# FFN pieces between the pieces of a recurrence, and a weight conversion moved between batch elements

## The chip, the cores and the metric

One core of a Trainium2 chip runs the whole program. The metric is the device time of one execution in microseconds (us). Where a ratio is given, it is the mean time of one kernel's fast runs over the mean of the other's fast runs of the same rounds, so it is not quite the ratio of the medians quoted beside it. On this one-core program a run counts as slow when it is over 1.5% above the fastest of its kernel.

One remark on reading the granted TensorE clock. The profile records its changes, and the first record lies some way into the profiled run; what comes before prints as 1.00. So the mean clock of a whole run is good to a few hundredths only.

## The reference, cut to what matters

```python
# 4 batch elements, 8 heads, 768 time steps, head size 40
for t in range(S):
    y[:, :, t] = einsum('bhd,bhde->bhe', r_t, state)
    Sa = einsum('bhde,bhe->bhd', state, a_t)
    state = state * w_t - einsum('bhd,bhe->bhde', Sa, b_t) + einsum('bhd,bhe->bhde', v_t, k_t)
x = y as (3072 tokens, 320)
h = x @ w_in                                  # 320 -> 2048
out = (h * clip(h + 3, 0, 6) / 6) @ w_out     # 2048 -> 320
```

A recurrence over time, then a feed-forward network (FFN) on each token.

## The kernel before

The kernel takes time in 6 groups of 128 steps. For each group and each of the 4 batch elements it does `prepare` (inputs turned, scaled, masked products), one `invert` for all four (a chain of small VectorE instructions), `off_diagonal`, then per element `step` (the state) and `outputs`, which ends in `yg`, the element's 128 finished tokens. An FFN of those tokens follows. The FFN weights arrive as float64 and are rounded to float32 on VectorE and GpSimd in 36 pieces; I call that the conversion.

The parts that matter here:

```python
def rounded(dst, n, loads):                       # one piece of the conversion
    raw = tmp.tile([P, DM, 2], U32, name="raw", tag="yg", bufs=2)   # yg's buffers!
    buf = ffn.tile([P, 3, DM], U32, name="parts", bufs=1)
    # ... DMA into raw, then 5 VectorE and 3 GpSimd instructions; the last, on GpSimd:
    nc.gpsimd.tensor_tensor(out=dst, in0=mf, in1=xf, op=ALU.mult)

def outputs(g, q, o):
    # ...
    yg = tmp.tile([P, NPR, P], F32, name="yg", tag="yg", bufs=2)

os_ = prepared(0)                # prepare x 4, invert, off_diagonal x 4
with behind():                   # everything in here gets a far lower priority
    load_weights()
for g in range(NG):
    def recur(q):
        step(q, os_[q])
        xt = outputs(g, q, os_[q])
        with behind():
            feed_forward(g, q, xt)
    if g + 1 < NG:
        os_ = prepared(g + 1, recur)     # recur(q) before each prepare(g + 1, q)
    else:
        for q in range(B):
            recur(q)
```

The framework builds each engine's instruction order from these priorities. I call that the built order; the prediction shows a wait of 39.8 us that VectorE's built order explains.

Of the kernel before, what the change touches and what calls it, by code (L numbers as in the profile page):

```python
# [15 lines left out]
P = 128  # L16
HP = 64
L = 32
NC = P // L
BEHIND = 1 << 20  # L20
# [10 lines left out]
def kernel(  # L31
# [147 lines left out]
    def load_weights():  # L179
        wi, wo = moe_w_in.bitcast(U32), moe_w_out.bitcast(U32)  # L180
        for i in range(2):
            for f in range(0, DFF, WC):
                rounded(win[:, i, f:f + WC], WC, [
                    (slice(p, p + n), wi[x:x + n, 2 * f:2 * (f + WC)])
                    for p, x, n in FEATURES[i]
                ])
        for f in range(0, DFF // 2, WC):
            rounded(win2[:, f:f + WC], WC, [
                (slice(i * SLOT + p, i * SLOT + p + n),
                 wi[x:x + n, i * DFF + 2 * f:i * DFF + 2 * (f + WC)])  # L190
                for i in range(2) for p, x, n in FEATURES[2]
            ])
        for j in range(NJ):
            rounded(wout[:, j, :], DM, [(slice(0, P), wo[j * P:(j + 1) * P, :])])

# [49 lines left out]
    def prepare(g, q, fc):  # L245
        o = {}
# [8 lines left out]
        wt = turn_pairs(WN)  # L255
        wv = wm[:].rearrange("p (r m i) -> p r m i", m=2, i=HP + 1)
# [25 lines left out]
        at = scaled(AN, gam, grp, "at", tag="at")  # L282
        bt = scaled(BN, rgam, tmp, "bt", tag="turned", bufs=4)
        kt = scaled(KN, rgam, tmp, "kt", tag="turned", bufs=4)
        o["at"] = at
# [3 lines left out]
        for n in range(NPR):  # L289
            nc.tensor.transpose(out=rg[:, n, :], in_=rgam[:, n, :], identity=ident[:])  # L290
        rgt = tmp.tile([P, H, D], F32, name="rgt", bufs=1)
# [17 lines left out]
        for pr in range(NPR):  # L309
            for s in range(2):  # L310
                rows = slice(SLOT * s, SLOT * s + D)
                nc.tensor.matmul(out=f[s][:, pr, :], lhsT=at[rows, pr, :], rhs=bt[rows, pr, :],
                                 start=True, stop=True)
        for s in range(2):
            for c in range(NC):
                cr = slice(c * L, (c + 1) * L)
                nc.scalar.activation(
                    out=fc[cr].rearrange("p (n s) t -> p n s t", s=2)
                    [:, q * NPR:(q + 1) * NPR, s, :],
                    in_=f[s][cr, :, cr], func=AF.Copy, scale=-1.0,  # L320
                )
                if c:
                    nc.scalar.activation(out=ft[cr, 4 * s:4 * s + 4, 0:c * L],  # L323
                                         in_=f[s][cr, :, 0:c * L], func=AF.Copy)
# [4 lines left out]
        masked(E, kt, at)  # L329
        ev = ps_any([P, H, D])  # L330
        for h in range(H):
            nc.tensor.matmul(out=ev[:, cross(h), :], lhsT=E[:, h % 2 * 4 + h // 2, :],  # L332
                             rhs=VN[:, cross(h), 0:D], start=True, stop=True)
        EV = grp.tile([P, H, D], F32, name="EV", tag="EV")
        nc.scalar.activation(out=EV[:], in_=ev[:], func=AF.Copy)
        o["EV"] = EV
        return o
# [31 lines left out]
    def off_diagonal(q, o):  # L369

        ft = o["F"]
        for s in range(2):
            wp = ps_any([P, 4, LW])
            for pr in range(NPR):
                nc.tensor.matmul(out=wp[0:LW, pr, :], lhsT=ft[:, 4 * s + pr, :],  # L375
                                 rhs=tinv[:, q * H + 2 * pr + s, L:P], start=True, stop=True)
            nc.scalar.activation(out=ft[0:LW, 4 * s:4 * s + 4, :], in_=wp[0:LW], func=AF.Copy)

# [6 lines left out]
    def step(q, o):  # L385
# [4 lines left out]
        for j in range(2):  # L390
            nc.tensor.transpose(out=sp[:, j, :],
                                in_=st[:, 2 * j:2 * j + 2, :].rearrange("p r d -> p (r d)"),
                                identity=ident[:])
        S = grp.tile([P, 2, P], F32, name="S", tag="S", bufs=2)
# [5 lines left out]
        for pr in range(NPR):  # L400
            for s in range(2):
                rows = slice(SLOT * s, SLOT * s + D)
                nc.tensor.matmul(out=rp[s][:, pr, :], lhsT=o["at"][rows, pr, :],  # L403
                                 rhs=st[rows, pr, 0:D], start=True, stop=True)
        for s in range(2):
            def places(x):
                return x[:].rearrange("p (n s c) e -> p n s c e", n=2, s=2)[:, :, s]
            nc.vector.tensor_tensor(
                out=places(R), in0=rp[s][:].rearrange("p (n c) e -> p n c e", n=2),
                in1=places(o["EV"]), op=ALU.add)  # L410

# [3 lines left out]
        for h in range(H):  # L415
            nc.tensor.matmul(out=up[:, cross(h), :], lhsT=tinv[:, q * H + h, :],  # L416
                             rhs=R[:, cross(h), :], start=(h == 0), stop=False,
                             skip_group_check=True)
        for c in range(NC):
            cr = slice(c * L, (c + 1) * L)  # L420
            if c:
                for h in range(H):
# [8 lines left out]
        for name, by in (("K", o["V"]), ("B", U)):  # L431
            for pr in range(NPR):
                for s in range(2):
# [5 lines left out]
                    )  # L439
        ssum = tmp.tile([P, NPR, D], F32, name="ssum")  # L440
# [4 lines left out]
    def outputs(g, q, o):  # L445
# [7 lines left out]
        RT, VT, UT = turned(RN), turned(o["V"]), turned(o["U"])  # L453
        m = {}
        for name, x in (("K", VT), ("B", UT)):
            m[name] = next_score()
            masked(m[name], x, RT)
        yg = tmp.tile([P, NPR, P], F32, name="yg", tag="yg", bufs=2)
        y = [ps_acc([P, 2, P]) for _ in range(2)]
        for c in range(2):  # L460
            for name in ("K", "B"):
                for n in range(2):
                    for s in range(2):
# [5 lines left out]
                            start=(name == "K" and n == 0), stop=False)  # L469
        for n in range(2):  # L470
            for s in range(2):
                for c in range(2):
# [4 lines left out]
                        rhs=RT[rows, 2 * n + s, :], start=False, stop=(n == 1))  # L477
        for c in range(2):
# [12 lines left out]
        return xt  # L491


    def feed_forward(g, q, xt):
# [3 lines left out]
        def expand(j0):  # L498

            hp = [bank("h", [P, NQ, P], 2) for _ in range(2)]  # L500
            for kt_ in range(2):
                for half in range(2):
                    for i in range(NQ):
# [4 lines left out]
                                         stop=False)  # L508
            for i in range(NQ):
# [5 lines left out]
            gts = []  # L515
# [7 lines left out]
            return gts  # L523

        def contract(j0, gts):
            for half in range(2):
                for i in range(NQ):
# [3 lines left out]
                                     stop=(j0 == HJ - NQ and half == 1 and i == NQ - 1))  # L531

        last = None
        for j0 in range(0, HJ, NQ):
            gts = expand(j0)
            if last:
                contract(*last)
            last = (j0, gts)
        contract(*last)
# [5 lines left out]
    @contextmanager  # L545
    def behind():

        p = tc.cur_priority
        tc.cur_priority = p + BEHIND
        yield  # L550
        tc.cur_priority = p

    def prepared(g, before=None):
        fc = inv.tile([P, NH, L], F32, name="fc")
        os_ = []
        for q in range(B):
            if before:
                before(q)
            os_.append(prepare(g, q, fc))
        invert(fc)  # L560
        for q, o in enumerate(os_):
            off_diagonal(q, o)
        return os_

    os_ = prepared(0)
    with behind():
        load_weights()
    for g in range(NG):
        def recur(q):
            step(q, os_[q])  # L570
            xt = outputs(g, q, os_[q])
            with behind():
                feed_forward(g, q, xt)

        if g + 1 < NG:
            os_ = prepared(g + 1, recur)
        else:
            for q in range(B):
                recur(q)
# [30 lines left out]
```

## Time and profile before

Before: 1406.8 us, the median of 3 runs (1405.1 to 1414.5); profiled span 1411.0. The span is best cut where an element's `yg` is done. "FFN" is the number of FFN matmuls started in a stretch, times their durations at full clock (0.223, 0.142 and 0.55 us for the three kinds, as in the prediction).

| stretch of the profiled run | us | granted clock | FFN, us at full clock |
|---|---|---|---|
| start to first `yg` | 225.2 | 0.62 | 0 |
| to the first `yg` of group 1 | 162.4 | 0.80 | 40.5 |
| rest of group 1 | 109.0 | 0.72 | 12.5 |
| groups 2 to 4 | 587.0 | 0.81 | 163 |
| group 5 | 164.0 | 0.91 | 74 |
| tail, FFNs alone | 163.4 | 1.00 | 147 |

The columns are start:end, length, busy us and records of PE, PEld, DVE, ACT and POOL, then granted clock, DMA share and GB/s:

```profile
225.20:387.60 162.40, 154.67 (x1368) 134.87 (x1368) 74.11 (x142) 41.84 (x104) 23.47 (x58) 0.80 0.15 26
496.60:1083.60 587.00, 551.90 (x4695) 476.69 (x4693) 265.78 (x486) 159.31 (x405) 77.28 (x200) 0.81 0.16 29
```

PE is busy 552 of 587 us in the middle, and yet runs there at a clock of 0.81.

### The profile page before, as it was taken

How to read it: one execution, taken by the hardware profiler on the slowest of the kernel's cores; microseconds unless marked ns; L12 is line 12 of the kernel's file. 1: busy time of each engine (PE TensorE's matmuls, PEld its weight loads, DVE VectorE, ACT ScalarE, POOL GpSimd, SP SyncE). 2: the span in 40 equal slices, each digit the busy share in tenths (PEclk: the TensorE clock that was granted, in tenths of full speed). 3: DMA queues.
4: the chain of work that ended last, by engine and by line, in shares of the span. 5: the costliest groups of instructions: out<-in, count | busy, mean ns of one | idle time of the engine just before them, and what ended most of it. 6: DMA issues, size and time to landing. Idle time of an engine off the chain costs nothing. (4 is left out here: it accounts for less than half of the span.)

```text
span 1411.0 us, 24203 instructions
## 1 busy us (share of the span) xinstructions
PE 1214.1 (86%) x10032; PEld 1041.7 (74%) x10032; DVE 582.2 (41%) x1113; ACT 327.2 (23%) x805; POOL 248.1 (18%) x503
## 2 busy tenths in 40 slices
PE   5732725999999998999999999898998999999998
PEld 4632615887888877888778888788787877777776
DVE  6577543337333474442733337433327312111111
ACT  2211200222322223322232221322222311111111
POOL 6455563111111111111111111111101000000000
PEclk9555656669957899886877759976999989899999
DMA  5221321221022210222102111011111000000000
GB/s 94 60 56 53 85 75 34 35 35 30 15 35 35 35 30 15 35 38 36 30 10 35 33 29 30 17 33 29 30 23 28 7 6 11 11 17 16 10 10 10
DMA packets 169885, 44.30 MB, mean 31 GB/s; under 512 B 155953, under 2 KB 165169, under 8 KB 169777
## 3 DMA queue, kind: packets, MB, share of 16 engines
q1 hardware_dynamic: 169776, 42.76, 15.1%
q8 instruction: 79, 1.29, 0.4%
q14 instruction: 30, 0.24, 0.1%
HBM read 34.08 MB, written 3.93 MB: 27 GB/s over the span
## 5 line engine op out<-in xcount | busy, mean ns | idle before, releaser
L528 PE MATMUL o<-wout,gt 128*128 128x320 f32 x768 | 240.4, 462 | 0.0
L505 PE MATMUL h<-xt,win 128*128 128x128 f32 x1536 | 210.8, 296 | 32.9 <-DVE gt L520 32.9
L505 PEld LDWEIGHTS h<-xt,win 128*128 128x128 f32 x1536 | 198.5, 208 | 41.8 <-DVE gt L520 36.3
L528 PEld LDWEIGHTS o<-wout,gt 128*128 128x128 f32 x768 | 145.6, 198 | 54.9 <-issue 2.4
L520 DVE SCALAR_TENSOR_TENSOR gt<-gt,h 128x512 f32<-128x512 f32 x96 | 62.6, 682 | 216.5 <-ACT gt L518 216.5
L238 DVE COPY_PREDICATED score<-mask,any 128x512 f32<-128x512 int32 x144 | 98.7, 721 | 102.8 <-PE any L235 102.7
L441 DVE TENSOR_TENSOR ssum<-any,state 128x160 f32<-128x160 f32 x24 | 7.8, 324 | 294.8 <-PE any L435 294.8
L518 ACT ACTIVATE gt<-h,three 128x512 f32<-128x512 f32 x96 | 61.0, 683 | 186.2 <-PE h L512 186.1
L235 PE MATMUL any<-cross 40*128 40x128 f32 x768 | 89.8, 342 | 2.8 <-DVE score L238 0.7
L235 PEld LDWEIGHTS any<-cross 40*128 40x128 f32 x768 | 81.1, 239 | 11.5 <-DVE score L238 6.0
L428 ACT ACTIVATE U<-acc 32x320 f32<-32x320 f32 x96 | 41.0, 428 | 206.4 <-PE acc L416 114.2
L332 PE MATMUL any<-VN,score 128*128 128x40 f32 x384 | 78.8, 374 | 9.8 <-DVE score L238 9.8
L423 PEld LDWEIGHTS acc<-U,ft 64*32 64x32 f32 (+2 forms) x1152 | 68.1, 145 | 25.4 <-ACT U L428 9.8
L332 PEld LDWEIGHTS any<-VN,score 128*128 128x128 f32 x384 | 74.4, 288 | 16.2 <-DVE score L238 11.9
L423 PE MATMUL acc<-U,ft 64*32 64x40 f32 (+2 forms) x1152 | 79.9, 242 | 1.3 <-ACT U L428 1.3
L375 PE MATMUL any<-tinv,ft 128*96 128x96 f32 x384 | 37.9, 265 | 46.0 <-POOL tinv L367 46.0
L235 PE MATMUL any<-at,kt 40*128 40x128 f32 x384 | 70.8, 341 | 3.5 <-ACT ft L323 3.5
L375 PEld LDWEIGHTS any<-tinv,ft 128*96 128x96 f32 x384 | 37.4, 181 | 47.4 <-POOL tinv L367 47.4
L403 PE MATMUL acc<-state,at 40*128 40x40 f32 x384 | 31.8, 292 | 44.5 <-DVE yg L479 44.5
L235 PEld LDWEIGHTS any<-at,kt 40*128 40x128 f32 x384 | 62.9, 245 | 7.4 <-ACT ft L323 6.2
L403 PEld LDWEIGHTS acc<-state,at 40*128 40x128 f32 x384 | 28.7, 198 | 50.6 <-DVE yg L479 47.4
L354 DVE TENSOR_TENSOR prod<-x 128x30 f32<-128x30 f32 (+9 forms) x180 | 60.5, 336 | 10.5 <-POOL x L347 5.6
(100 smaller groups left out, 1748.0 us busy)
## 6 DMA issues: line engine op xcount, KB each, us to landing
raw<-in_moe_w_out_dram SPq DMA_DIRECT2D x16, 320.0 KB
WN<-in_w_dram SPq DMA_DIRECT2D x24, 160.0 KB
VN<-in_v_dram SPq DMA_DIRECT2D x96, 40.0 KB
AN<-in_a_dram SPq DMA_DIRECT2D x24, 160.0 KB
KN<-in_k_dram SPq DMA_DIRECT2D x24, 160.0 KB
BN<-in_b_dram SPq DMA_DIRECT2D x24, 160.0 KB
RN<-in_r_dram SPq DMA_DIRECT2D x96, 40.0 KB
out_dram<-ob SPq DMA_DIRECT2D x24, 160.0 KB
```

The lines of the kernel that those rows point to most:

```text
L235: nc.tensor.matmul(out=o[s][:, n, :], lhsT=lhs[rows, n, :], rhs=rhs[rows, n, :], start=True, stop=True)
L238: nc.vector.copy_predicated(out=x[:, 4 * s:4 * s + 4, :], mask=mask4, data=o[s][:])
L332: nc.tensor.matmul(out=ev[:, cross(h), :], lhsT=E[:, h % 2 * 4 + h // 2, :], rhs=VN[:, cross(h), 0:D], start=True, stop=True)
L354: nc.vector.tensor_tensor(out=pv, in0=_ap(x[:], (k + 1) * L + k, [[L, n], [0, k]]), in1=_ap(x[:], k * L, [[0, n], [1, k]]), op=ALU.mult,)
L375: nc.tensor.matmul(out=wp[0:LW, pr, :], lhsT=ft[:, 4 * s + pr, :], rhs=tinv[:, q * H + 2 * pr + s, L:P], start=True, stop=True)
L403: nc.tensor.matmul(out=rp[s][:, pr, :], lhsT=o["at"][rows, pr, :], rhs=st[rows, pr, 0:D], start=True, stop=True)
L423: nc.tensor.matmul(out=up[cr, cross(h), :], lhsT=o["F"][0:c * L, h % 2 * 4 + h // 2, (c - 1) * L:c * L], rhs=U[0:c * L, cross(h), 0:D], st ...
L428: nc.scalar.activation(out=U[cr, :, 0:D], in_=up[cr], func=AF.Copy, scale=-1.0)
L505: nc.tensor.matmul(out=hp[half][:, i, :], lhsT=win[:, kt_, j * P:(j + 1) * P], rhs=xt[:, kt_, :], start=(kt_ == 0 and i == 0), stop=False)
L518: nc.scalar.activation(out=gt[:], in_=hp[half][:], func=AF.Relu, bias=three[:], scale=1.0)
L520: nc.vector.scalar_tensor_tensor(out=gt[:], in0=gt[:], scalar=6.0, in1=hp[half][:], op0=ALU.min, op1=ALU.mult)
L528: nc.tensor.matmul(out=op[:], lhsT=gts[half][:, i, :], rhs=wout[:, half * HJ + j0 + i, :], start=(j0 == 0 and half == 0 and i == 0), stop= ...
```

## The change

Intent: issue the FFN in pieces of about a microsecond between the pieces of the recurrence, as much FFN time as recurrence time, from group 1 on; and convert the weights between the elements of the first group instead of ahead of its first `yg`. No arithmetic changes. The core of the diff, cut (the order of two loops, in `outputs` and in the FFN's first product, changes with it):

```diff
 def load_weights():                      # now a generator, one yield for each piece;
-    for i in range(2): ...               # pieces in the order in which the FFN needs them
+            yield
 def prepare / step / outputs / off_diagonal:     # generators: yield <ns of TensorE work>
     at = scaled(AN, gam, grp, "at", tag="at")
+    yield 440
     # f products
+    yield 900
     masked(E, kt, at)
+    yield 900
     # ev products (128-row weights, 40 columns)
+    yield 1800
     # at * state
+    yield 900
     # tinv * R (128-row weights, 40 columns)
+    yield 1800
     # ... and some 20 more
 def feed_forward: expand yields after every 4 full-height matmuls (once after the 8 of half height), contract after every 2
-    with behind():
-        feed_forward(g, q, xt)
+    fill.append(feed_forward(g, q, xt))
+fill = deque()
+def spend(debt):
+    while debt > 0 and fill:
+        try: debt -= next(fill[0])
+        except StopIteration: fill.popleft()
+    return min(debt, 0)
+def issue(*stages, share=1.0):
+    debt = 0
+    for stage in stages:
+        for ns in stage:
+            debt = spend(debt + share * ns)
+weights = load_weights()
+for g in range(-1, NG):
+    for q in range(B):
+        if g >= 0: issue(step(q, os_[q]), outputs(g, q, os_[q]), share=g > 0)
+        if fc:     issue(prepare(g + 1, q, fc, ahead[q]), share=g > 0)
+        if g == 0:
+            for _ in range(9): next(weights)
+    if fc: invert(fc); ... off_diagonal
+spend(float("inf"))
```

## The prediction

> **What bounds the kernel now.** I read, in this order: the page's busy slices and TensorE clock, the busy time by stretches of the span, the same stretches for the FFN's second matmul (L528) alone, the chain that ended last in order of time, and the waits. The page first:
>
> ```profile
> PE 1214.1 (86%) x10032; PEld 1041.7 (74%) x10032; DVE 582.2 (41%) x1113; ACT 327.2 (23%) x805; POOL 248.1 (18%) x503
> PE   5732725999999998999999999898998999999998
> DVE  6577543337333474442733337433327312111111
> PEclk9555656669957899886877759976999989899999
> ```
>
> TensorE is busy nine tenths of nearly every slice after the eighth, yet its clock there is anything from 0.5 to 1.0: the busy share hides how much of it is time at half clock. VectorE is busiest in the first seven slices, where TensorE is idle half the time.
>
> I cut the span at the moments when a batch element's output product (`yg`, L479, two VectorE instructions each) is done. There are 24: 6 time groups of 4 batch elements. Stretches, columns being length, then busy us (and records) of PE, PEld, DVE, ACT, POOL, then granted clock, DMA share and GB/s:
>
> ```profile
> 146.90:225.20 78.30, 27.39 (x184) 23.81 (x180) 39.99 (x92) 7.46 (x22) 48.66 (x61) 0.54 0.28 77
> 463.10:496.60 33.50, 33.35 (x297) 27.90 (x296) 13.31 (x20) 9.20 (x27) 5.31 (x16) 0.80 0.22 37
> 632.00:670.70 38.70, 38.70 (x317) 34.58 (x316) 13.17 (x20) 9.71 (x28) 5.38 (x16) 0.65 0.22 36
> 994.20:1038.60 44.40, 41.33 (x405) 34.99 (x404) 15.18 (x24) 12.02 (x31) 5.21 (x15) 1.00 0.16 32
> 1247.60:1411.00 163.40, 148.29 (x1028) 122.93 (x1027) 20.56 (x32) 24.16 (x41) 0.00 (x0) 1.00 0.04 12
> ```
>
> The three in the middle are each one batch element of the recurrence (step, outputs, preparation for the next group). They differ in FFN and clock. The same two stretches for L528 alone (PE, PEld, clock):
>
> ```profile
> 463.10:496.60 33.50, 7.62 (x20) 4.30 (x20) 0.80 0.22 37
> 994.20:1038.60 44.40, 9.88 (x32) 5.68 (x32) 1.00 0.16 32
> ```
>
> An fp32 matmul leaves two records. So the stretch from 463.10 holds 10 L528 matmuls and, by the same view, no L505 or L512; the one from 994.20 holds 16 L528, 32 L505 and 16 L512, one whole FFN. What does an FFN cost at full clock? The chain of work in order of time (start, length, what), from the tail, where FFNs run alone:
>
> ```profile
> 1259.75 8.81 PE o L528 x32
> 1268.56 3.57 PE h L505 x32
> 1272.13 1.14 PE h L512 x16
> 1274.71 3.84 PE h L505 x32
> 1278.55 1.09 PE h L512 x16
> 1279.64 8.81 PE o L528 x32
> ```
>
> The period is 1279.64 - 1259.75 = 19.9 us, of which 8.81 + 3.57 + 1.14 + 3.84 + 1.09 = 18.45 us is matmul and 1.4 us a wait for the activation. Hence the recurrence's own part: 44.4 - 18.45 = 26.0 us at clock 1.00; 33.5 - 10 x 0.55 = 28.0 us at 0.80 (8.81/16 = 0.55 each); the stretch from 632.00, with 4.7 us of FFN by count, leaves 34 us at 0.65. **This is the finding: the 13 us of FFN more between the second stretch and the fourth lengthened the batch element by only 11 us; the recurrence's part costs 26 us with a whole FFN beside it and 28 to 34 with a quarter of one.** With little FFN beside it, TensorE runs at half clock part of the time, and in the last 163 us 8 FFNs run alone.
>
> At the start another thing binds. The waits, and the weight conversion's last instruction (durations min/median/max, first and last start):
>
> ```profile
> PE acc L403 <- DVE yg L479: 44.5, 6, 39.8
> L177 POOL TENSOR_TENSOR win<-parts x20: 722/728/815, 23.6 to 146.9; 128x256 f32<-128x256 f32 x20
> L177 POOL TENSOR_TENSOR wout<-parts x16: 852/857/864, 151.3 to 228.8; 128x320 f32<-128x320 f32 x16
> L479 DVE TENSOR_TENSOR yg<-acc,gam x48: 369/414/426, 224.4 to 1247.2; 128x256 f32<-128x256 f32 x48
> ```
>
> TensorE waits 39.8 us at once for the first `yg`. Its inputs were ready at about 158 us (L474's first start is 157.4), but it runs at 224.4, after the weights. The code says why: `raw`, the weights' staging tile, shares `yg`'s two buffers, and in VectorE's built order 19 conversion pieces stand between the end of the first matrix inversion and that `yg`.
>
> **What the Trainium skill says.** "TensorE: Matmul & The Clock Gate", Part 1: the array is throttled by default, and activity over windows of about 3.4 us releases it; the granted share is one half or all. The trace agrees: the stretch 95 to 101 us, with no matmul at all, reads 0.50, the tail 1.00, the mixtures lie between. The page speaks of idle gaps; here the stretch from 632.00 is busy throughout by the records and still gets 0.65. Same page, "Engine queue depths": VectorE and ScalarE queues are strict FIFO; the 39.8 us wait above agrees. "Perfetto Trace Analysis", opening note: matmul busy time is a bad metric since matmuls are pipelined; agreed, as 33.35 busy of 33.50 still had room.
>
> **The change part by part.** No instruction of the arithmetic goes or comes: 768 L505, 384 L512 and 384 L528 matmuls in both built programs, 36 conversion pieces in both. Only order changes. I counted, in both built orders, the FFN matmuls between the batch elements' last output matmuls, and turned them into us at full clock (0.223 for L505, 0.142 for L512, 0.55 for L528):
>
> ```
>               before                    after
> group 0:       0.0  1.4  4.3  4.4        0.0  0.9  3.1  4.2
> group 1:      30.6  1.8  5.3  5.5       22.5  8.2 16.8 18.3
> group 2:      27.2  5.0  5.5  4.6       31.3 13.9 18.3 18.3
> group 3:      26.5  5.5  4.6  1.8       31.7 12.6 18.3 18.3
> group 4:      30.2  4.6 15.8 18.3       31.1 13.2 18.3 18.3
> group 5:      29.5  2.2 23.2 18.3       31.9  7.7 11.5 11.2
> tail:        163                        59.3
> ```
>
> Step 1, the start. Before, the four preparations' VectorE work ends at 86.6 us with 8 conversion pieces among it, the inversion runs from 86.5 to 131.4 us with more pieces among it, and from there L375 (8.2 us), step and outputs take 27 us to 158. After, no piece stands in VectorE's order before the first `yg`. I take 2 us off each preparation: inversion from about 79. It has 60 small VectorE instructions of about 0.34 us, two transposes of 2 us and some 3 us on POOL: 28 us, so 107, then the 27 us less a few for the pieces among them: first `yg` at about 132 instead of 225.
>
> Step 2, conversion. It now starts after the next preparation's VectorE work, near 142. Before, 36 pieces took from 6.9 to 229 us: 6.2 us each, and 5.2 us each in the denser second half ((228.8 - 151.3)/15). A piece is a chain through VectorE and POOL over one `parts` buffer, so pieces don't overlap. At 5.5: 198 us, end near 340. The built order has 8, 9 and 9 pieces before the three following `yg`, the remaining 10 inside the second inversion, and TensorE's L375 behind FFN matmuls that need nearly the last piece. Add L375, step and outputs, some 22 us: first `yg` of group 1 at 362, against 387.6. Gain 26 us, with 10 us less FFN done.
>
> Step 3, rest of group 1: FFN 8.2 + 16.8 + 18.3 = 43.3 plus 3 x 26.5 = 123 (before 109 with 12.6 of FFN).
>
> Step 4, groups 2 to 4: four elements of 26.5 (the mean, at a clock of 0.93 or more, of the last four elements that prepare, whose L375 is in it) are 106, FFN 80.9 to 81.8, and 3 for dips of the clock: 190 each, 570 (before 587 with 150 of FFN, now 244).
>
> Step 5, group 5: the first element 31.9 + 26 + 2 = 60; three without preparation, 17.4 us at full clock and 20.4 at 0.83 before, are taken as 22 with 30.4 us of FFN: 97. Together 157 (before 164).
>
> Step 6, tail: 59.3 x 19.9/18.45 = 64, and 8 for the last activation and store: 72 (before 163.4).
>
> Sum: 362 + 123 + 570 + 157 + 72 = 1284. I say 1280.
>
> **The rivals.** (a) Work is only moved: PE was already busy, so what leaves the tail lengthens the middle one for one, and the time stays at about 1390 to 1400. For it: busy at 95 to 99% in the middle. Against: the 26, 28 and 34 us above. (b) The conversion becomes the bound: it starts 135 us later, and at 6.5 us a piece ends near 376, holding TensorE in order behind it; then about 1320. For it: pieces among inversion steps took some 6 us before. (c) Finer mixing makes new waits: only one pair of `h` banks and one `o` bank, and a matmul that waits for its activation now holds the recurrence behind it. In the tail such waits are 1.4 us per FFN; if each of 20 FFNs cost 2 to 3 us more, 1330. Against: in the stretch from 994.20, so mixed already, TensorE idled only 3 us. (d) Better: mixing also hides those 3 us, and the conversion runs at 4.6 us a piece, as in its undisturbed passages: about 1235.
>
> **Range and chances.** (b) and (c) set the top, 1330; (d) the bottom, 1235. Faster than 1379 (2%) fails only if (a) holds or (b) and (c) both strike hard: 0.93 faster, 0.05 within 2%, 0.02 slower.
>
> **What would show it.** Step 1: first `yg` near 132 and no 40 us wait of L403. Step 2: L177 from about 145 to 340. Steps 3 and 4: groups 2 to 4 near 190 us each with a clock over 0.95 and no FFN-free element. Step 6: a tail near 72 us. I am wrong if the middle's clock stays near 0.8 in spite of the FFN beside it, if L177 goes on past 375, or if matmuls gain waits for `gt` of several us per element.

## The result, and the profile after

The changed kernel takes 1373.2 us, the median of 4 runs (1369.1 to 1376.3); the kernel before beside it 1408.0 (1405.1 to 1414.5). The ratio is 0.9745, 95% interval 0.9702 to 0.9788: faster by 2.5%, where 1280 us and 9% were predicted, and outside the predicted range of 1235 to 1330. The profiled execution (span 1367.4) is a fast one. Cut at the same moments:

| stretch | before | predicted | after | after less predicted |
|---|---|---|---|---|
| to first `yg` | 225.2 | 132 | 129.2 | -3 |
| to the first `yg` of group 1 | 387.6 | 362 | 399.3 | +37 (moment) |
| rest of group 1 | 109.0 | 123 | 124.2 | +1 |
| groups 2 to 4 | 587.0 | 570 | 624.1 | +54 |
| group 5 | 164.0 | 157 | 152.8 | -4 |
| tail | 163.4 | 72 | 67.0 | -5 |
| sum from the second row on | 1411.0 | 1284 | 1367.4 | +83 |

Four terms are right within 5 us; two carry the whole miss. The lines of the program have new numbers: the FFN's matmuls L505, L512 and L528 are now L528, L536 and L551, the masked products L235 are L240, and the conversion's end is L177 in both. In the trace, the middle and the tail (columns as above):

```profile
129.20:399.30 270.10, 209.99 (x1411) 176.07 (x1409) 147.41 (x326) 47.96 (x123) 117.13 (x172) 0.60 0.24 57
523.50:1147.60 624.10, 602.95 (x5203) 505.20 (x5202) 258.19 (x469) 167.00 (x409) 71.65 (x189) 0.87 0.15 27
1300.40:1367.40 67.00, 58.96 (x398) 48.23 (x397) 7.76 (x13) 9.34 (x16) 0.00 (x0) 1.00 0.04 14
```

The middle gained 0.06 in clock, from 0.81 to 0.87, and not the 0.14 and more that the prediction assumed ("a clock over 0.95"). It now holds 243 us of FFN instead of 163: 80 us more work for 37 us more time, so part of the prediction's finding stands. By an estimate from the same records, some 14 us of the saving are idle time of TensorE that was filled (35 us before, 21 now), and some 31 us are the half-clock time that went (222 us before, 160 now; half of it counts as lost).

Where the clock goes is best seen in two neighbouring elements of group 2, one from 638.0 to 680.3 us, the other from 680.3 to 741.8 (columns as above):

```profile
638.00:680.30 42.30, 40.30 (x405) 33.64 (x404) 15.07 (x25) 11.91 (x31) 5.21 (x15) 1.00 0.20 33
680.30:741.80 61.50, 60.46 (x405) 50.39 (x404) 15.12 (x25) 12.02 (x31) 5.21 (x15) 0.64 0.13 23
688.30:732.70 44.40, 43.95 (x247) 37.00 (x248) 5.28 (x10) 9.04 (x24) 2.11 (x7) 0.50 0.13 22
```

Both hold 405 matmul records, one at a clock of 1.00 in 42.3 us, one at 0.64 in 61.5 us; the third line is a single stretch of 44.4 us at exactly half clock, in which PE is busy 43.95 us. The groups of instructions in the first element, then in the second (line, operation, names, shapes, count, busy us, mean ns, idle before):

```profile
L551 PE MATMUL o<-wout,gt 128*128 128x320 f32 x32 | 10.1, 442 | 0.0
L528 PE MATMUL h<-xt,win 128*128 128x128 f32 x64 | 9.4, 287 | 0.9 <-DVE gt L543 0.9
...
L343 PE MATMUL any<-VN,score 128*128 128x40 f32 x16 | 2.1, 278 | 0.0
L430 PE MATMUL acc<-R,tinv 128*128 128x40 f32 x16 | 1.9, 277 | 0.0
...
L486 PE MATMUL acc<-score,Kt 128*64 128x128 f32 x16 | 1.3, 285 | 0.0
```

```profile
L528 PE MATMUL h<-xt,win 128*128 128x128 f32 x64 | 15.0, 402 | 0.4 <-DVE gt L543 0.4
L551 PE MATMUL o<-wout,gt 128*128 128x320 f32 x32 | 14.1, 582 | 0.0
L343 PE MATMUL any<-VN,score 128*128 128x40 f32 x16 | 3.7, 406 | 0.0
L430 PE MATMUL acc<-R,tinv 128*128 128x40 f32 x16 | 3.5, 405 | 0.0
...
L486 PE MATMUL acc<-score,Kt 128*64 128x128 f32 x16 | 1.3, 285 | 0.0
```

The counts agree line by line. Only the durations differ, and L486, outside the half-clock stretch, keeps its 1.3 us. The idle column shows 0.9 us at most: waits do not make up the 19 us. So the loss in the middle is clock, in an engine that the profile shows busy nearly throughout.

At the start, the conversion's last instruction (durations min/median/max, first and last start), and the waits:

```profile
L177 POOL TENSOR_TENSOR win<-parts x20: 718/728/1587, 141.3 to 294.0; 128x256 f32<-128x256 f32 x20
L177 POOL TENSOR_TENSOR wout<-parts x16: 858/866/952, 300.1 to 376.0; 128x320 f32<-128x320 f32 x16
```

```profile
PE o L551 <- POOL wout L177: 29.1, 9, 14.3
...
PE h L528 <- DVE gt L543: 18.2, 12, 4.1
```

The conversion runs from 141.3 to 376.0 us, (376.0 - 141.3) / 35 = 6.7 us for each piece, and the FFN's second product (L551) waits 29.1 us for `wout`. The 40 us wait of the first state product for `yg` is gone, as predicted. The last of these waits in the kernel before:

```profile
PE h L505 <- DVE gt L520: 32.9, 17, 4.4
```

The waits of FFN matmuls for their activation fell from 32.9 us to 18.2: the prediction's rival (c), new waits by finer mixing, is not what happened. While the conversion runs, from 141.3 to 376.0 us, VectorE waits for TensorE like this (in total us, times, longest us):

```profile
DVE score L243 <- PE any L240: 25.9, 8, 12.5
DVE ssum L458 <- PE any L451: 22.8, 3, 12.9
DVE R L422 <- PE acc L416: 11.0, 3, 6.7
```

That is 59.7 us, 1.7 for each of the 35 intervals between pieces; in the stretch from which the prediction took its rate (151.3 to 229 us of the kernel before) the same view gives 0.7 us in all. What VectorE waits for holds up the conversion pieces that stand behind it in its built order.

### The profile page after: what moved, and what is told of

It reads as the page before. It is cut to its first block, busy times and chain, and to the rows that moved or that the text cites. A ratio compares the mean times of both kernels' runs of the same rounds, so it can differ in the third digit from the quotient of the medians.

```text
span 1367.4 us, 24180 instructions
## 1 busy us (share of the span) xinstructions
PE 1221.7 (89%) x10032; PEld 1023.1 (75%) x10032; DVE 587.7 (43%) x1113; ACT 327.0 (24%) x805; POOL 244.7 (18%) x503
## 5 line engine op out<-in xcount | busy, mean ns | idle before, releaser
L551 PE MATMUL o<-wout,gt 128*128 128x320 f32 x768 | 266.3, 484 | 29.1 <-POOL wout L177 29.1
L528 PE MATMUL h<-xt,win 128*128 128x128 f32 x1536 | 243.8, 314 | 27.3 <-DVE gt L543 18.2
L528 PEld LDWEIGHTS h<-xt,win 128*128 128x128 f32 x1536 | 218.7, 221 | 42.1 <-DVE gt L543 21.8
L551 PEld LDWEIGHTS o<-wout,gt 128*128 128x128 f32 x768 | 147.6, 208 | 84.9 <-POOL wout L177 32.9
L343 PEld LDWEIGHTS any<-VN,score 128*128 128x128 f32 x384 | 78.5, 301 | 7.4 <-issue 5.3
L343 PE MATMUL any<-VN,score 128*128 128x40 f32 x384 | 81.1, 383 | 0.2 <-DVE score L243 0.2
L240 PE MATMUL any<-at,kt 40*128 40x128 f32 x384 | 74.0, 355 | 5.6 <-ACT ft L333 4.5
L536 PE MATMUL h<-xt,win 64*128 64x128 f32 x768 | 76.6, 315 | 0.8 <-POOL win L177 0.8
L240 PEld LDWEIGHTS any<-at,kt 40*128 40x128 f32 x384 | 65.2, 256 | 14.9 <-ACT ft L333 9.9
L365 DVE TENSOR_TENSOR prod<-x 128x30 f32<-128x30 f32 (+9 forms) x180 | 64.7, 360 | 10.5 <-POOL x L358 5.5
L536 PEld LDWEIGHTS h<-xt,win 64*128 64x128 f32 x768 | 61.1, 210 | 10.8 <-issue 5.2
L240 PE MATMUL any<-cross 40*128 40x128 f32 x768 | 65.7, 312 | 1.6 <-ACT cross L467 1.3
L439 PEld LDWEIGHTS acc<-U,ft 64*32 64x32 f32 (+2 forms) x1152 | 52.8, 121 | 18.9 <-issue 10.2
L467 ACT ACTIVATE cross<-any 128x512 f32<-128x512 f32 x72 | 42.1, 597 | 98.8 <-PE any L228 87.2
L370 DVE TENSOR_TENSOR x<-x,prod 128x30 f32<-128x30 f32 (+9 forms) x180 | 62.8, 349 | 5.3
```

The lines of the kernel that those rows point to most:

```text
L240: nc.tensor.matmul(out=o[s][:, n, :], lhsT=lhs[rows, n, :], rhs=rhs[rows, n, :], start=True, stop=True)
L343: nc.tensor.matmul(out=ev[:, cross(h), :], lhsT=E[:, h % 2 * 4 + h // 2, :], rhs=VN[:, cross(h), 0:D], start=True, stop=True)
L365: nc.vector.tensor_tensor(out=pv, in0=_ap(x[:], (k + 1) * L + k, [[L, n], [0, k]]), in1=_ap(x[:], k * L, [[0, n], [1, k]]), op=ALU.mult,)
L370: nc.vector.tensor_tensor(out=rest, in0=rest, in1=pv, op=ALU.add)
L439: nc.tensor.matmul(out=up[cr, cross(h), :], lhsT=o["F"][0:c * L, h % 2 * 4 + h // 2, (c - 1) * L:c * L], rhs=U[0:c * L, cross(h), 0:D], st ...
L528: nc.tensor.matmul(out=hp[half][:, i, :], lhsT=win[:, kt_, j * P:(j + 1) * P], rhs=xt[:, kt_, :], start=(kt_ == 0 and i == 0), stop=False)
```

## The experiments

Twelve kernels ran. All gave a correct result except the two probes, which compute something else.

### Each part of the change alone

The pieces alone: the changed kernel, with the weights converted as before.

```diff
+if g < 0:
+    tc.cur_priority = p + (1 << 20); load_weights(); tc.cur_priority = p
-        if g == 0:
-            for _ in range(9): next(weights)
```

> The changed kernel with the weights converted as before (all 36 pieces right after the first preparation, lowest priority), FFN pieces kept. Theory: converting between the batch elements gained nothing, because VectorE's in-order queue waits there for a half-clock TensorE; then the first output product comes near 225 us again, the first one of group 1 near 388, and the rest is as in the changed kernel (968 us): 1350 to 1370, within 1% of the changed kernel. Rival (the prediction's step 2 had the sign right): the placing is worth some 26 us, and this kernel is at 1390 to 1400.

Measured: 1378.6 us median of 4 (1340.0 to 1380.9; the run at 1340.0 had a mean clock of 0.881, the others 0.822 to 0.849), the kernel before in the same rounds 1414.4 (1397.4 to 1415.6). Only one run, that at 1340.0, counts as fast, and the profile is of a slow one (1378.3). The expected 1350 to 1370 was missed by 9 us. First `yg` at 224.1, first `yg` of group 1 at 392.7, middle 621.0 us at 0.88, tail 66.5.

The weights alone: the kernel before, with the conversion between the elements.

```diff
-with behind():
-    load_weights()
+        if g == 0:                       # after each element of the first group
+            for _ in range(9): next(weights)
```

(The first group's FFNs are issued after the conversion, at the low priority of before.)

> The kernel before with only the weights converted between the batch elements (9 pieces after each of group 0; group 0's FFNs are issued after them, at lowest priority as before). Theory: first output product near 130, first of group 1 near 395 to 400, the rest as before (1023 us): 1410 to 1425, no gain. Rival: the placing gains 26 us alone: 1380 to 1385.

Measured: 1434.5 us (1421.1 to 1446.8), ratio to before 1.0119 (1.0008 to 1.0230): if anything slower, and 10 us above the range expected. First `yg` at 136.0, but the first of group 1 at 412.3 instead of 387.6.

The two runs agree, by the ranges of all runs: the pieces carry the gain, and the moved conversion gains some 90 us at the first `yg` and has lost all of it one group later, with either way of issuing the FFN (399.3 against 392.7, and 412.3 against 387.6).

### Where the FFN's share is put

If the clock falls where the recurrence issues its 40-column products, then more FFN beside these and none beside the rest should keep it up, at about the same total. Only the numbers in the yields change:

```diff
-        yield 440   # after turned inputs, transposes        +        yield 0
-        yield 900   # after f products                       +        yield 3600
-        yield 900   # after masked(E, kt, at)                +        yield 3600
-        yield 1800  # after ev products                      +        yield 3200
-        yield 900   # after at * state                       +        yield 1800
-        yield 450   # after y products                       +        yield 0
```

> The changed kernel with the same FFN per batch element, but its share moved beside the preparation's L321, L240, L343 and the step's first matmuls (3600, 3600, 3200, then 1800, 1800), none beside the transposes and the outputs but 900 per masked product. Theory: the granted clock falls to one half once per element in just that stretch, because those matmuls count little as activity; with FFN beside them it stays up: mean clock of groups 2 to 4 from 0.87 to 0.95 or more, those groups from 637 to 580 to 600 us, total 1310 to 1335. Rival 1 (only the amount of FFN per element sets the clock): clock 0.87, total within 1% of 1370. Rival 2 (the lost time is waits of TensorE in the finer mixing): clumps of FFN relieve or worsen it by a few us, clock unchanged.

(The 637 us named there is not the cut of my tables, which gives 624.1 for groups 2 to 4.) The opposite placement puts 0 where this has much, and 900 or 1800 where it has 0:

> The opposite of the former: FFN beside the transposes and outputs (900 to 1800 each), none beside L321, L240, L343 and the step's first matmuls. Theory: the clock falls earlier and for longer: mean of groups 2 to 4 at 0.80 or below, those groups 670 us or more, total 1385 to 1420. Rival 1 (amount alone): within 1% of 1370.

Measured: the first 1329.6 us median (1302.7, 1324.9, 1334.4, 1343.3), all below the changed kernel's lowest run of 1369.1; the second 1418.3 (1415.8 to 1422.2), ratio to before 1.0074 (1.0004 to 1.0145), so the whole gain of the change was gone. The middle of the first, whose profiled run is its fastest, then one of its elements, then the middle of the second:

```profile
513.60:1106.50 592.90, 566.97 (x5359) 476.47 (x5358) 260.39 (x475) 170.49 (x417) 71.75 (x190) 0.97 0.17 29
667.50:711.20 43.70, 42.71 (x418) 35.27 (x417) 15.66 (x26) 13.01 (x34) 5.72 (x17) 1.00 0.20 36
```

```profile
545.30:1205.50 660.20, 638.11 (x5318) 535.43 (x5318) 260.99 (x473) 170.31 (x416) 71.80 (x190) 0.84 0.14 26
```

The two placements hold nearly the same FFN in the middle, 265 and 260 us, and one takes 67 us longer: the clock is 0.97 in one and 0.84 in the other, and 0.87 in the changed kernel. TensorE idles 26, 22 and 21 us in these stretches, so idle time is not the difference. For the second I had expected 0.80 or below and 670 us or more: right in direction, too strong. One thing besides the place differs: the first puts up to 3.6 us of FFN into one lump, the second and the changed kernel at most 1.8. No run separates place and size of the lumps. The 592.9 us hold 22 us more of FFN than the changed kernel's 624.1. Take these 22 us away and about 571 us are left, worked out from these two runs: the prediction's 570, once its clock is there. So the sum of that step was right, and the clock was the term that failed. This is the fastest execution of the four; the other three took 22 to 41 us longer and left no trace.

### Which matmuls lose the clock, and which bring it back

A probe runs one form of matmul after the other, each between 110 full-size ones (128 rows, 128 columns of weights, 128 columns moving).

```python
full(110)
for i in range(100):      # 128 x 128 weights, 40 columns moving
    nc.tensor.matmul(out=o[i % 2][:, 0:40], lhsT=ys[:, 0:P], rhs=xs[:, 0:40], start=True, stop=True)
full(110)
for i in range(150):      # 40-row weights in alternating halves, 128 columns moving
    nc.tensor.matmul(**rowpair(i, 40, P, P))
# ... and so on for each form, then for mixes
```

> Not the computation (its output is zero): TensorE alone, one form of matmul at a time for some 20 to 40 us, a stretch of 110 full 128x128x128 matmuls between each two. Theory: granted clock 1.0 in stretches of full matmuls, of 320-column ones and of the column pairs; 0.5 in stretches of 128x128 weights with 40 columns moving (L343, L430), of 40-row pairs (L321, L240, L416), of 96-row ones with 32 columns (L439) and probably of the 64-row pairs (L536); transposes unknown. Mixed stretches: a quarter of full matmuls is not enough for 1.0, a half is for the 40-column form. Rival: every form keeps the clock at 1.0 as long as TensorE has no idle time, so all stretches read 1.0 and the drops in the kernels come from short waits.

Measured (one run): the stretch of 40 columns moving, the 40-row pairs with 128 moving, the transposes, then the 40-row pairs with 40 moving, and the mix of three quarters of the first form and one quarter full-size:

```profile
31.80:69.40 37.60, 37.60 (x203) 37.60 (x203) 0.00 (x0) 0.00 (x0) 0.58 0.00 0
96.70:113.70 17.00, 17.00 (x302) 16.86 (x301) 0.00 (x0) 0.00 (x0) 1.00 0.01 2
180.10:193.30 13.20, 13.20 (x124) 13.20 (x122) 0.00 (x0) 0.00 (x0) 1.00 0.00 1
294.70:321.90 27.20, 27.20 (x302) 27.10 (x301) 0.00 (x0) 0.00 (x0) 0.60 0.00 1
406.30:428.40 22.10, 22.10 (x200) 22.10 (x200) 0.00 (x0) 0.00 (x0) 1.00 0.00 1
```

I had expected row pairs and the small 96 x 32 form to fall too, and they did not: only the two forms with 40 columns moving under 128 columns of weights fell to half. And one quarter of full-size matmuls was enough to keep the full clock: 22.1 us / 200 records = 110 ns for each. In the changed kernel, though, half of the work is FFN and the clock still stays down for up to 44 us. The second probe therefore starts every stretch from half clock, with 70 of the 40-column matmuls ahead of it.

```diff
-full(110)
+cool()       # 70 matmuls, 128 x 128 weights, 40 columns moving
```

> A probe with a wrong output on purpose: stretches of one form of matmul each, every one entered from half clock (70 products with 40 columns moving go ahead of it). Theory, from the records of the changed kernel, where the clock came back only after full FFN matmuls or full-width products: mixes of a quarter, a half and three quarters of full matmuls return to 1.0 only at a half or more; 40-row products with 128 columns moving, 64-row pairs, transposes and column pairs stay at 0.5 until the full matmuls. Rival (what keeps the clock also raises it): all the forms that kept 1.00 when entered from full clock return to 1.0 within two records (7 us), and only those with 40 columns moving stay at 0.5.

Measured (one run): mixes with one quarter, one half and three quarters of full-size matmuls, then 40-row pairs with 128 moving, 64-row pairs, transposes:

```profile
34.50:85.60 51.10, 51.10 (x241) 51.10 (x242) 0.00 (x0) 0.00 (x0) 1.00 0.00 1
115.50:166.70 51.20, 51.20 (x242) 51.20 (x242) 0.00 (x0) 0.00 (x0) 1.00 0.00 1
196.60:225.00 28.40, 28.40 (x240) 28.40 (x241) 0.00 (x0) 0.00 (x0) 1.00 0.01 1
249.60:282.00 32.40, 32.40 (x302) 32.16 (x301) 0.00 (x0) 0.00 (x0) 0.50 0.00 1
384.90:403.30 18.40, 18.40 (x302) 18.27 (x301) 0.00 (x0) 0.00 (x0) 0.92 0.01 2
428.50:446.90 18.40, 18.40 (x155) 18.40 (x154) 0.00 (x0) 0.00 (x0) 0.90 0.01 2
```

The first record of the clock in this run is at 200.1 us, so the 1.00 of the first two lines is the empty reading named above; their own rates decide. One quarter: 51.1 us / 240 matmul records = 213 ns. One half: 51.2 / 240 = 213 ns. The same mixes took 110 ns when entered from full clock. Three quarters: 28.4 / 240 = 118 ns, and the first record of the clock, a rise to 1.0, falls into that stretch. The 40-row pairs, 57 ns in the first probe (17.0 / 300), stayed at 0.50 and took 108 ns. The 64-row pairs and the transposes came back within 4 us. Two more stretches, entered from full clock: 40-row products that are not in alternating halves fell to half (0.54 over their 48.2 us), and 64 columns of weights with 40 moving kept 1.00.

So there are three kinds, in these two runs: forms that bring the clock back, forms that keep it but don't bring it back (40-row pairs; mixes with a quarter or half of full-size work), and forms that lose it. My expectation was wrong for half full-size work, which I thought enough, and for 64-row pairs, transposes and column pairs, which I thought too little; the rival was wrong for 40-row pairs and the first two mixes.

Where does the clock of the changed kernel itself fall? In groups 2 to 4 its records show 13 falls to half, 160 of the 624 us in all (41 of 593 and 205 of 660 in the two placements). No record of half clock is shorter than 3.4 us, so I look at the 3.4 us ahead of each fall. Only two falls, at 609.8 and 1026.2 us, follow the 40-column products (L343, L430), with no FFN among them. Three follow a pause of TensorE of 2 us or more. The other eight, with 137 of the 160 us, follow 40-row products (L321, L240) with at most 0.9 us of FFN beside them, and in seven of the eight TensorE also paused for 0.4 to 1.1 us. This stands ahead of the 44.4 us that begin at 688.3 (start, length, what, idle before):

```profile
684.54 0.43 PE L551 MATMUL o<-wout,gt 128*128 128x320 f32 x1
685.57 0.63 PE L298 MATMUL any<-ident,rgam 128*128 128x128 f32 x4 [0.59 <-DVE at L284]
686.12 1.36 PE L321 MATMUL any<-bt,at 40*128 40x128 f32 x13
...
687.66 0.72 PE L240 MATMUL any<-at,kt 40*128 40x128 f32 x5
```

So the fall is mostly not beside the 40-column products that I had suspected, but in the preparation, where the equal share left 3.3 us without FFN in this case. Pairs of 40-row products in alternating halves kept the clock in the first probe, and 40-row products all in one half lost it in the second; whether it is the pause, the incomplete pairing or the missing FFN that costs it here, no run separates. The way back is clearer: cut into 13 pieces of 3.41 us, the 44.4 us hold 0.85 to 2.30 us of FFN in each of the first twelve, and 2.41 us in the last, after which the clock is full again. That fits the second probe, where half full-size work did not bring the clock back and three quarters did. It is a reading of one kernel's records, not a threshold: in the opposite placement the clock came back after pieces with less. What the two placement runs show is that moving the FFN, lumps and all, changes the clock and with it the time.

### Why the first group takes so long

My first theory was this: the TensorE at half clock in the first group holds VectorE's queue, and the conversion with it. It is tested by work that nobody needs: full-size matmuls between the pieces of the first group's recurrence.

```diff
+def useless():
+    while True:
+        hp = bank("h", [P, 4, P], 2)
+        for i in range(4):
+            nc.tensor.matmul(out=hp[:, i, :], lhsT=tinv[:, i, :], rhs=tinv[:, 4 + i, :],
+                             start=(i == 0), stop=(i == 3))
+        yield 900
-issue(..., share=g > 0)
+issue(..., share=g >= 0, fill=fill if g else dummy)
```

> The change, with useless full-size matmuls issued between the pieces of the first group's recurrence, where no FFN can run yet. Theory (a TensorE at half clock holds VectorE's in-order queue and through it the conversion): granted clock in the first group rises from about 0.58 to over 0.85, the conversion ends before 360 us instead of 376, first yg of group 1 comes at about 360 to 375 instead of 399, total 1335 to 1350 although over 50 us of matmuls are added. Rival (the start is bound by the VectorE work or by work on TensorE itself): clock rises, but first yg of group 1 stays at 399 or comes later, total 1373 or more.

Measured: 1370.6 us (1358.5 to 1381.1), around the changed kernel's 1369.1 to 1376.3, where the theory had put 1335 to 1350. The useless matmuls alone by stretches (PE, PEld, clock):

```profile
0.00:138.90 138.90, 14.18 (x103) 12.43 (x104) 0.67 0.20 33
138.90:303.00 164.10, 80.56 (x481) 70.25 (x480) 0.82 0.29 70
303.00:394.60 91.60, 9.52 (x60) 8.55 (x59) 0.85 0.18 44
```

104 us of useless work cost nothing in total, though the first `yg` came 10 us later (14 us of them lay ahead of it). The clock from the first to the last `yg` of the first group rose from 0.56 to 0.82, and the conversion ran from 151.7 to 352.0 us, 5.7 us for each piece instead of 6.7; VectorE's waits for TensorE in that time fell from 59.7 us to 17.8 (11.3, 3.3, 2.8 and 0.4 in the same view), 1.2 us less for each piece. But the first `yg` of group 1 came at 394.6, hardly before 399.3. I put that down to FFN work that had found room in the first group and now lay behind it: the last stretch held 33 us of FFN instead of 12. So the theory holds for the rate of the conversion, and it did not pay; the run leaves open whether the rate mattered for the end.

The second theory concerns `raw`. The weight pieces take their buffers in turn with `yg`. That order is fixed when they are issued: in the kernel before, the pieces issued ahead of the first `yg` must go first (35 of the 36 had); in the changed one, every piece issued behind it must wait. Three kernels let `raw` share the buffers of `gt`, the FFN's gate products, which are four instead of two, and change nothing else but one buffer less for `ob`:

```diff
-raw = tmp.tile([P, DM, 2], U32, name="raw", tag="yg", bufs=2)
+raw = ffn.tile([P, DM, 2], U32, name="raw", tag="gt", bufs=4)
-gt = ffn.tile([P, NQ, P], F32, name="gt", bufs=4)
+gt = ffn.tile([P, NQ, P], F32, name="gt", tag="gt", bufs=4)
-ob = ffn.tile([P, DM], F32, name="ob", bufs=2)
+ob = ffn.tile([P, DM], F32, name="ob", bufs=1)      # to make it fit
```

On the pieces alone:

> The change with the weights converted as before (as in the run of the pieces alone), but the float32 image of the weight pieces shares the buffers of the FFN's gate products instead of those of the output product yg. Theory: in the run of the pieces alone the first yg (224 us) had to wait for almost all of the conversion because it took its buffers in turn with the weight pieces; freed of that, first yg at about 185 us, first yg of group 1 at 345 to 355 instead of 393.3, total about 1330 against 1378.6. Rival: the wait only moves, since the matmuls of the first group still queue behind VectorE's conversions: first yg of group 1 stays at 385 or more and the total within 1% of 1378.

On the changed kernel:

> The changed kernel with one edit: the float32 image of a weight piece takes its buffers from the FFN's gate products instead of the output product yg. Theory (in the changed kernel the conversion is late because VectorE's queue stands behind products of a half-clock TensorE, not because of the shared buffers): first yg of group 1 at 385 to 405 us as in the changed kernel (399.3), total 1355 to 1385. Rival (the 37 us that the prediction missed are the shared buffers): first yg of group 1 at 355 to 370, total about 1335.

On the kernel before:

> The kernel before with that one edit of buffers and nothing of the change. Theory: the 126 us in which TensorE idles in its first 225 us are the shared buffers, so first yg falls from 225 to about 180 and first yg of group 1 from 388 to about 350; but what is gained at the start is not all kept, since the FFN left over for the end stays: total 1365 to 1385 against 1410. Rival: within 1% of before.

| `raw` apart from `yg`, on | median (range), us | ratio to before | pieces converted ahead of first `yg` | first `yg` | first `yg` of group 1 |
|---|---|---|---|---|---|
| the pieces alone | 1326.3 (1314.0-1332.5) | 0.9390 | 29 (was 35) | 177.1 (was 224.1) | 363.3 (was 392.7) |
| the changed kernel | 1317.6 (1298.3-1330.1) | 0.9268 | 28 (was 0) | 169.5 (was 129.2) | 349.7 (was 399.3) |
| the kernel before | 1389.1 (1382.8-1393.4) | 0.9861 | 29 (was 35) | 177.6 (was 225.2) | 355.1 (was 387.6) |

The last row is unclear (interval 0.9793 to 0.9928), and 4 us above the range expected. That `raw` also got four buffers in place of two was not tested alone; but the pieces did not come faster by it (5.9 to 6.3 us each in these three runs, 5.9 in the kernel before), only earlier or later.

In the first row, the first `yg` of group 1 came 8 us after the 345 to 355 that I expected. The second row is where my theory fell. I had put the first `yg` of group 1 at 385 to 405 and the total at 1355 to 1385, since I thought VectorE's queue was the cause; the rival said 355 to 370, and it came at 349.7. The conversion in that run:

```profile
L177 POOL TENSOR_TENSOR win<-parts x20: 719/727/1583, 23.7 to 126.7; 128x256 f32<-128x256 f32 x20
L177 POOL TENSOR_TENSOR wout<-parts x16: 859/862/877, 131.1 to 236.4; 128x320 f32<-128x320 f32 x16
```

It starts at 23.7 us and not at 141.3, although the program issues it between the elements just as the changed kernel does. With `raw` and `yg` apart, nothing in the buffers ties the pieces to the first `yg`, and the build moved them forward. Ahead of the first `yg` TensorE idled 82 us then, 126 in the kernel before and 51 in the changed one; but up to the first `yg` of group 1 it idled 95, 134 and 111. Either order imposed by the shared buffers costs one of the two ends; the free one is a compromise that is better at the end that counts. The middle of that run is the changed kernel's, unmoved:

```profile
466.50:1090.90 624.40, 603.07 (x5201) 505.57 (x5201) 258.09 (x468) 166.95 (x409) 71.61 (x189) 0.87 0.16 27
```

624.4 us at 0.87 against 624.1 at 0.87. So the two losses are separate ones, and each has its own remedy. By medians one remedy took 44 us off the changed kernel, the other 56, and both together (below) 82 to 84.

### Both remedies together

The moved shares with `raw` in the buffers of `gt`, once with the weights ahead:

> The FFN shares moved beside the 40-column products and the preparation (as in the run that took 1302 to 1343 us), weights converted ahead, and the float32 image in the FFN's buffers. If the two gains add: 1302 to 1343 less about 45 us, that is 1255 to 1300 us, groups 2 to 4 at a granted clock over 0.93. Rival: the time saved at the start is not kept, because the clock in the middle decides: over 1300.

and once with the weights between the elements:

> The moved shares (the run of 1302 to 1343 us) with weights converted between the elements as in the change, and the float32 image in the FFN's buffers: against the same with the weights converted ahead (1272 to 1299 us) this tells what the place of the conversion is worth once the buffers are not shared. Theory (between the elements the conversion is slower, because VectorE waits for TensorE in its order): first yg of group 1 at 385 to 405, total 1300 to 1340, slower than converted ahead by 20 to 40 us. Rival: both alike within 1%.

Measured: 1288.8 us (1271.7 to 1299.0), ratio to before 0.9048 (0.8972 to 0.9123), and 1291.7 (1278.6 to 1297.5), ratio 0.9169 (0.9072 to 0.9265). The first ratio rests on two fast runs of four; the means of the fast runs, 1276.5 and 1289.9, are 1.1% apart, the ranges overlap, and I count them as not told apart. In the middle the clock was 0.94 (a slow run) and 0.96. My expectation that conversion between the elements would be slower by 20 to 40 us failed, for the reason just shown (28 pieces stand ahead of the first `yg` in one, 29 in the other). Both beat the kernel before and the changed one in every run, and they need no more than other numbers in the yields and another ring of buffers.

## Why the prediction was right or wrong

**Step 1, the start: right, part by part.** First `yg` at 129.2 against "about 132", and the 40 us wait is gone; the inversion ran from 76.9 to 104.2 us, where 79 to 107 was said.

**Step 2, the conversion: a term mis-sized.** Its start was right (near 142; 141.3 measured). The rate "at 5.5" was not: 6.7 us for each piece, so the end lay at 376 instead of 340, and the first `yg` of group 1 at 399.3 instead of 362. Rival (b) had these numbers (6.5 a piece, an end near 376), and I gave it too little weight. I took the rate from a stretch in which VectorE waited for TensorE for 0.7 us in all, although the new place puts the pieces among instructions that wait for a TensorE at half clock: 59.7 us of such waits, 1.7 us for each piece. The useless matmuls bear this out: with a faster clock there, and 17.8 us of such waits, a piece took 5.7 us instead of 6.7. The rest of the sum held: from the end of the conversion to the `yg` 22 us were said, and it took 22. What the step did not see at all is that the shared buffers, which the prediction itself names as the cause of the old wait, make a new one in the other direction. With them separated, the first `yg` of group 1 comes at 349.7.

**Step 3, rest of group 1: right in sum** (124.2 against 123), in part by luck: two elements at a clock of 1.00 took 5 and 3 us less than the 26.5 us for the recurrence's part, and the third, at 0.75, took 10 more.

**Step 4, groups 2 to 4: wrong, and the largest term.** The step says "and 3 for dips of the clock: 190 each, 570". The dips were not 3 us for each group: TensorE stood at half clock for 160 us of the middle, the mean clock was 0.87, and an element's part of the recurrence took (624.1 - 243)/12 = 31.8 us instead of 27.2. The middle took 624.1. The work in the step was counted rightly, as the run at 0.97 shows (about 571 us for the same FFN). What failed is the inference from the kernel before: three elements with one whole FFN (18.2 us) beside them ran there at 0.96 to 1.00, so I took the *amount* of FFN as what keeps the clock. The same trace held the answer, which I passed over. The 26.5 us are a mean over elements with "a clock of 0.93 or more", and among the last that prepare this leaves out one:

```profile
921.70:994.20 72.50, 67.71 (x487) 59.37 (x485) 23.58 (x32) 18.81 (x52) 9.08 (x26) 0.69 0.18 33
```

It had 16.6 us of FFN and a clock of 0.69, with only 2 us of FFN in the 27 us that it stood at half clock (932.1 to 959.4). Two elements of group 5, with 19.6 and 21.5 us of FFN, ran at 0.83 and 0.86. The placement runs, with nearly the same amount, give 0.97 and 0.84: it is where, and in what lumps, the FFN lies. And the probes suggest why an average is not enough, as what keeps a clock is less than what brings it back.

**Steps 5 and 6: right in sum** (152.8 against 157, 67.0 against 72). In step 5 two errors cancel: the first element took 71.0 us where 60 was said, the other three 81.9 where 97 was.

**The rivals.** (a), work only moved, is not it: 80 us of FFN entered the middle for 37 us. (b) is what happened at the start, in the kernel as it was changed. (c), new waits, is refuted by the wait table. The prediction's 1284, with 37 us at the start and 54 in the middle added and 8 taken off for the other terms, is the 1367 of the profiled run. I had named the sign for this (the middle's clock "near 0.8") without giving it a rival of its own, which is why the range was too narrow.

The gain expected of the tail was real: 163.4 - 67.0 = 96 us. It was given back as 37 us in the middle (624.1 - 587.0), 15 in the rest of group 1 and 12 up to the first `yg` of group 1, while 11 were gained in group 5. With one more decimal, 96.4 - 37.1 - 15.2 - 11.7 + 11.2 = 43.6, the 1411.0 - 1367.4 of the two profiled runs.

Open: why the same code runs at different clocks from one execution to the next (1302.7 to 1343.3 us for the moved shares), which property of a matmul makes it count for the clock (the forms tested here sort by no single one that I can name), and whether the place of the FFN or the size of its lumps does more.

## What to carry to other kernels

When filler work is mixed in to hold the TensorE clock, look in the records for the place where the clock falls and put the filler there (the run that did so used lumps of up to 3.6 us); an even share over everything did not hold it here, and half of full-size work did not bring it back in the probe. Before moving a preparatory stage past a result, look at whose buffers it shares: a shared ring fixes an order in both directions, and moving the stage turned one wait into another here. And read matmul busy time together with the granted clock, by stretches with the same instruction counts, as busy alone hid 19 us between two elements with the same 405 records.

## What the Trainium skill lacked or had wrong

- "TensorE: Matmul & The Clock Gate", Part 1, says that the full clock comes after at least one busy window of about 3.4 us, and gives "no PE-idle gaps" over about 3.4 us as the rule for keeping it. Here that was not enough: a stretch of 44.4 us with 43.95 us busy stayed at half clock, and in the second probe a mix with half full-size matmuls ran 51.2 us at 213 ns for each record, without a gap, where the same mix took 110 ns when entered from full clock. The part has nothing on which matmuls count, nor on keeping being easier than bringing back. Its statement that only one half or all is granted agrees with every record of these runs.
- The same page, Part 4, says of transposes that the full clock "doesn't engage" for them. In the second probe fp32 transposes entered from half clock came back to full within 4 us (18.4 us at a mean of 0.90), and in the first probe they held 1.00 for 13 us.
- No page has the case of two kinds of data in one ring of buffers: here it cost a wait of 40 us in one order, and a start of the conversion later by 118 us (141.3 against 23.7) in the other.
